# The stretch between the last logits and the expert products: written order, u and spp in halves, accumulators summed early

## The chip, the cores and the metric

The kernel runs on one core of a Trainium2 chip. The metric is the device time of one execution in microseconds. Three executions of the kernel before were timed and a further one was profiled; all times below that are points in the trace count from the profiled execution's first instruction. PE is TensorE's matmul, PEld its weight load, DVE VectorE, ACT ScalarE, POOL GpSimd, SP the engine whose queue issues every DMA here.

## The reference

Three layers follow each other in float32.

```python
# 1. attention, 4 x 8 heads x 576 x 64, local mask for heads 0-3, strided for 4-7 -> x (2304, 512)
# 2. h = x @ w_in;  g = h * sigmoid(1.702 h);  y = g @ w_out          (2304, 2048) and back
# 3. soft mixture of 8 experts with 4 slots each, on y:
logits = y @ phi                                  # (2304, 32)
d = softmax(logits, axis=0)                       # over tokens
slot_input = (d.T @ y).reshape(8, 4, 512)
slot_out[e] = maximum(slot_input[e] @ w1[e], 0) @ w2[e]        # 512 -> 1024 -> 512
c = softmax(logits, axis=1)                       # over slots
return c @ slot_out                               # (2304, 512)
```

The maximum over all tokens and the sum of the exponentials over all tokens are known only when the last token's logits are.

## The kernel before

The tokens are worked on in five chunks, four of 512 and a last one of 256. `moe_step` runs over 80 steps (c, f): chunk c, column block f of 128 of the 2048 hidden columns. A step makes `h` (12 matmuls in `gemm1`, L321), turns it into `g` with ACT and DVE (L324, L325) and transposes `g` in blocks of 32 with DVE (`g_transpose`, L348). The product with `w_out` is never made: `wp` is `w_out @ phi`, so the logits come from `g` directly (`logits`, L340, four f at a time, in four column tiles of 32), and `slot_input` is made as (d.T @ g) @ w_out.

`post(c)` keeps a running softmax over tokens. It copies the logits to `l4` (L388), sums and repeats them over the four column tiles with the matrix `rep` (`lr`, L391), takes the maximum (`nmx`, L393, L396), the exponentials (L402) and their block transposes `dT` (L404), the factor `al` by which earlier sums shrink (L408), and the running sum `z`. Then `u` = d.T @ g is made in four PSUM banks, one for each row group of 32 of PE, with 32x32 tiles (L435), and added into the accumulators `acc` with the factor `al` (L453). In the last chunk the four parts are not added into `acc`; they are copied out (L445), and `ut` sums old accumulators and new parts in PE with two weights, `selz[:, 1]` (selector times 1/z times `al`, L442) and `selz[:, 0]` (selector times 1/z, L446).

Behind that, at the end of the program: `ut` is transposed to `uts` (L590), `spp` is its product with `w_out`, which lies as 16 row blocks in `ex[0]` to `ex[3]` (L594), `acc_s` its copy in two halves (L596, L597), `sip` the sum over the four column tiles, transposed (L600), and `si` the slot inputs (L602). `expand1(G, n)` makes hidden columns of expert group G, 512 at a time, in four steps kt with the tiles `ex[4 + 8G + 4n + kt]` (L641), `hidden_t` transposes them (L652) and DVE spreads them into `hz` (L657). `expand2(half, n)` multiplies by the second expert weights `ex[20]` to `ex[35]` (L671) for three column ranges of 256, 128 and 128, `slot_out` splits the result, and `combine` multiplies it by the token weights (L688), copies the result out of PSUM (L691, L693) and issues the output DMA (L694).

The token weights are made by `combine_weights(c)` (L463 to L471: six DVE operations with one ACT exponential after the second), split by `combine_split` (L620, L621) and transposed by `combine_t` (`ctp`, L627, one transpose for each of 18 token blocks).

`load_ex` issues the 36 loads of 1 MB (L489) in a fixed order; each waits in SP's queue until the place it goes to is free. Before, nine of them go out at step (3, 2), two at (4, 1), two into places of `gT` at (4, 4), eight into places of `w_in` as its tiles are used up in chunk 4, one after the last step, and the rest from the u of the last chunk on, behind `spp` and the expert products that free their places.

Within these rules the order on each engine is found by a scheduler: among the instructions whose inputs are ready in its own simulation of the program it takes the one that was written first. `keep_busy(n)` issues n matmuls whose result nobody reads (L78).

## Time and profile before

| | |
|---|---|
| time, three executions | 438.43 us median (436.42 to 438.57) |
| time of the profiled execution | 439.01 us |
| span of the profiled execution | 437.1 us |
| mean granted TensorE clock | 0.985 |
| PE busy | 411.6 us (94%) |
| DVE, ACT, POOL busy | 263.6, 194.1, 77.5 us |
| HBM read, written | 71.34, 8.91 MB |

The span reaches from the first to the last instruction; 1.9 us of the profiled execution's time lie outside it. A granted clock of 1.00 is 2.4 GHz, 0.50 is 1.2 GHz. Busy time of PE is that of pipelined matmuls with modelled ends, so a busy PE is not a PE at its peak.

### The profile page before, as it was taken

To read this page: it belongs to the slowest core of one execution; us is meant where nothing else is said; L and a number is where in the kernel's file an instruction comes from. 1 tells how busy PE (TensorE), PEld (TensorE's weight loads), DVE (VectorE), ACT (ScalarE), POOL (GpSimd) and SP (SyncE) were. 2 spreads that over 40 slices of the span, in tenths; PEclk is the share of its full clock that TensorE was granted. 3 is DMA by queue.
4 is the path that set the end of the run, shared out by engine and by line. 5 is a ranking of instruction groups with operands and counts; after the bars stand their busy time and mean duration, and the time that the engine had idled before them with its cause. 6 is when DMAs were issued, how large, how long until landed. Compare 5 with 4: busy or idle time off the path is not lost.

```text
span 437.1 us, 10068 instructions
## 1 busy us (share of the span) xinstructions
PE 411.6 (94%) x4085; PEld 280.5 (64%) x4085; DVE 263.6 (60%) x564; ACT 194.1 (44%) x640; POOL 77.5 (18%) x96
## 2 busy tenths in 40 slices
PE   8978998998899999999999999999999999799992
PEld 4646575655467767777676776775777797243681
DVE  2789989998996555555557456546545465422141
ACT  3874867766664653555553436331221222220131
POOL 0454545454531110100110001000000000010000
PEclk9999999999989999999999999999999999899997
DMA  8957677676752130213411101693001899859998
GB/s 253 357 170 243 223 208 251 228 242 218 233 183 76 47 101 1 92 37 97 154 40 60 38 1 37 214 410 147 1 0 39 343 349 329 307 212 427 421 358 255
DMA packets 25614, 80.90 MB, mean 185 GB/s; under 512 B 2144, under 2 KB 9440, under 8 KB 21472
## 3 DMA queue, kind: packets, MB, share of 16 engines
q1 hardware_dynamic: 25568, 80.26, 52.5%
q8 instruction: 32, 0.52, 0.5%
q14 instruction: 14, 0.11, 0.1%
HBM read 71.34 MB, written 8.91 MB: 184 GB/s over the span
## 4 chain that ended last, share of the span: by engine, by line
PE 73%; DVE 8%; ACT 7%; POOL 4%; issue 3%; DMA 2%; SPq 0%; ACTq 0%; POOLq 0%; DVEq 0%
PE h L321 39%; PE u L435 5%; PE s L163 4%; PE lg L340 4%; PE op L671 4%; ACT ts L181 3%; PE hp L641 3%; PE ptp L199 3%; PE av L218 3%; DVE wc L264 2%; POOL ts L184 2%; PE fp L688 2%; POOL wc L262 2%; DVE wc L265 1%; DMA raw<-wraw 1%
## 5 line engine op out<-in xcount | busy, mean ns | idle before, releaser
L321 PE MATMUL h<-x,wi 128*128 128x512 f32 (+1 forms) x960 | 225.2, 381 | 4.3 <-POOL wi L273 1.7
L321 PEld LDWEIGHTS h<-x,wi 128*128 128x128 f32 x960 | 162.2, 189 | 53.8 <-issue 13.8
L325 DVE SCALAR_TENSOR_TENSOR gT<-gT,h 128x512 f32<-128x512 f32 (+1 forms) x64 | 40.6, 634 | 62.1 <-ACT gT L324 61.5
L324 ACT ACTIVATE gT<-h 128x512 f32<-128x512 f32 (+1 forms) x64 | 35.5, 555 | 68.2 <-PE h L321 66.6
L181 ACT ACTIVATE ts<-ts,nmx 128x64 f32<-128x64 f32 (+1 forms) x120 | 41.6, 349 | 28.6 <-DVE nmx L176 28.2
L184 POOL TENSOR_TENSOR ts<-ts,sm 128x384 f32<-128x384 f32 (+2 forms) x32 | 27.9, 872 | 139.2 <-DVE sm L183 65.5
L348 DVE STREAM_TRANSPOSE gT<-gT 128x512 f32<-128x512 f32 (+1 forms) x64 | 41.0, 649 | 0.9
L262 POOL TENSOR_SCALAR wc<-wc 128x512 f32<-128x512 f32 x32 | 25.0, 781 | 29.7 <-ACT wc L261 27.2
L340 PE MATMUL lg<-gT,wp 128*32 128x512 f32 (+1 forms) x128 | 27.2, 564 | 0.3 <-ACT wp L297 0.3
L264 DVE SCALAR_TENSOR_TENSOR wc<-raw,wc 128x512 uint32<-128x512 uint32 x32 | 26.0, 816 | 0.4
L263 DVE TENSOR_SCALAR wc<-wc 128x512 uint32<-128x512 uint32 x32 | 20.3, 635 | 7.9 <-POOL wc L262 7.9
L163 PE MATMUL s<-qk 64*64 64x96 f32 (+1 forms) x552 | 25.0, 235 | 0.0
L163 PEld LDWEIGHTS s<-qk 64*64 64x64 f32 x552 | 20.9, 133 | 6.3 <-issue 5.3
L243 ACT CAST x<-av 128x320 fp32r<-128x320 f32 (+20 forms) x54 | 19.1, 394 | 12.7 <-DVE x L244 9.1
L273 POOL TENSOR_TENSOR wi<-wc,wi 128x512 fp32r<-128x512 f32 x16 | 22.0, 1376 | 14.9 <-ACT wi L272 14.7
L265 DVE SCALAR_TENSOR_TENSOR wc<-raw,wc 128x512 uint32<-128x512 uint32 x32 | 24.4, 763 | 0.3
L261 ACT ACTIVATE wc<-raw 128x512 f32<-128x512 f32 x32 | 21.7, 678 | 4.3 <-DMA raw<-wraw 3.8
L182 DVE TENSOR_SCALAR sm<-sm 128x5 f32<-128x5 f32 (+2 forms) x32 | 6.8, 213 | 27.5 <-ACT ts L181 27.5
L435 PE MATMUL u<-gT,dT 32*32 32x512 f32 x576 | 21.0, 618 | 2.1 <-DVE z L410 2.1
L199 PE MATMUL ptp<-cs,ts 128*96 128x128 f32 (+1 forms) x120 | 18.2, 286 | 4.9 <-POOL ts L184 4.5
L181 ACT ACTIVATION_READ_ACCUMULATOR ts<-ts,nmx 128x1 f32 x120 | 22.6, 188 | 0.0
L699 POOL MEMSET hz<- 128x512 f32 x4 | 2.1, 560 | 112.1 <-PE spp L594 112.1
(124 smaller groups left out, 467.7 us busy)
## 6 DMA issues: line engine op xcount, KB each, us to landing
ex<-wexp SPq DMA_DIRECT2D x28, 1024.0 KB, 8.4
raw<-wraw SPq DMA_DIRECT2D x32, 512.0 KB, 4.2
qk<-lqk SPq DMA_DIRECT2D x8, 592.0 KB, 5.1
wo_scr<-wc SPq DMA_DIRECT2D x16, 256.0 KB, 2.8
ex<-wo_scr SPq DMA_DIRECT2D x4, 1024.0 KB, 9.2
gT<-wexp SPq DMA_DIRECT2D x4, 1024.0 KB, 7.0
qk<-sqk SPq DMA_DIRECT2D x6, 604.0 KB, 4.2
v<-lv SPq DMA_DIRECT2D x8, 432.0 KB, 4.8
```

The source lines that it names most:

```text
L163: nc.tensor.matmul(sp[hs, u], t[hs, qo:qo + 64], t[hs, ko + qo:ko + qo + nk], start=not early, stop=not early or u == nt - 1)
L181: nc.scalar.activation(ts[:, u], src[:, u], AF.Exp, scale=sc, bias=nmx[:, u:u + 1], accum_out=sm[:, u:u + 1])
L184: nc.gpsimd.tensor_tensor(ts, ts, sm[:, :nt].unsqueeze(2).to_broadcast([P, nt, nk]), op=ALU.mult)
L199: nc.tensor.transpose(ptp[:nk, u - a], src, ident)
L262: nc.gpsimd.tensor_scalar(t, t, F64_LARGE, F64_SMALL, op0=ALU.min, op1=ALU.max)
L264: nc.vector.scalar_tensor_tensor(u, raw[:, :, 1], 0xC0000000, u, op0=ALU.bitwise_and, op1=ALU.bitwise_or)
L321: nc.tensor.matmul(h[:, :N], w[:, we, 128 * kt:128 * kt + 128], x[xe][:, kt, :N], start=n == 0, stop=n == 11)
L324: nc.scalar.activation(g[:, :N], h[:, :N], AF.Tanh, scale=0.851)
L325: nc.vector.scalar_tensor_tensor(g[:, :N], g[:, :N], 1.0, h[:, :N], op0=ALU.add, op1=ALU.mult)
L340: nc.tensor.matmul(lgs[c][32 * j:32 * j + 32, :N], wp[:, f0 + j, :], gs[c, f0 + j][:, :N], start=f0 == 0, stop=f0 == NF - 4)
L348: nc.vector.transpose(t_slots(c)[:, f, :N], gs[c, f][:, :N])
L435: nc.tensor.matmul(us[a][32 * j:32 * j + 32, :].rearrange("p (t f) -> p t f", f=32), dT[q, 32 * b:32 * b + 32], gT[q, :, 32 * b:32 * b + 3 ...
```

## The change

The last chunk gets a function of its own, `post_last`, and `post` keeps the other four.

- At step (4, 6) `fold_acc` sums the four accumulators with `sel` into one bank `ua` and copies it to the place of `l4` and `dT`. The place of `acc` then takes a load (`load_ex(None, acc)`), so this load stands earlier in SP's queue and the last call that used to load the 36th tile loads nothing.
- From the last logits to `hidden_t(1, 0)` PE, DVE and ACT issue the instructions emitted in this region in the order in which they are written. Where instructions emitted outside of the region fall among them is left to the scheduler.
- `keep_busy(6)` behind the logits becomes 2 ahead of them, 1 ahead of `lr` and 4 ahead of `u`.
- `u` is made in two halves of 256 columns in eight banks. Each half is copied out, summed by `sel` into `ut_0` and `ut_1`, added to `ua` times `al` and transposed by DVE on its own.
- `spp` is made in two column halves, in the order given by `rows`. The factor 1/z moves from `selz` to the copies of `spp` (`scaled`). `sip` and `si` come in two halves; the second (`slot_in(1)`) is issued inside `expand1(0, 0)` behind kt = 0.
- `combine_weights(4)` and the split and transposes of chunks 0 and 1 stand in the region at the place where they are written, behind `hidden_t(0, 0)` and ahead of `expand1(1, 0)`; those of chunks 2 to 4 are written among `expand2(0, 5)` to `(0, 7)` as before.
- `uts`, `acc_s`, `c4t` and `cT0` have no tiles of their own any more; they lie in freed places.

```diff
-        if last:
-            zi = keep.tile([P, 1], F32, name="zi")
-            nc.vector.tensor_scalar(zi, st["z"], 1e-9, 2.0, op0=ALU.add, op1=ALU.mult)
-            nc.vector.reciprocal(zi, zi)
-            selz = keep.tile([P, 2, NS], F32, name="selz")
-            nc.vector.tensor_scalar_mul(selz[:, 0], sel, zi)
-            nc.vector.tensor_scalar_mul(selz[:, 1], selz[:, 0], al)
...
-            ut = mtile("ut")
-            for a in range(4):
-                nc.tensor.matmul(ut[32 * a:32 * a + 32, :], selz[:, 1], acc[:, a], start=True, stop=False)
-            for a in range(4):
-                u = slots[NF + a]
-                (nc.scalar.copy if a % 2 else nc.vector.tensor_copy)(u, us[a])
-                nc.tensor.matmul(ut[32 * a:32 * a + 32, :], selz[:, 0], u, start=False, stop=True)
-            st["ut"] = ut
-            return
...
+    def fold_acc():
+        st["l4"] = sp_["p"].tile([P, 512], F32, tag="l4", name="l4_last")
+        st["dT"] = sp_["p"].tile([P, 512], F32, tag="dT", name="dT_last")
+        ua = mtile("ua")
+        for a in range(4):
+            nc.tensor.matmul(ua[32 * a:32 * a + 32, :], sel, acc[:, a], start=True, stop=True)
+        st["ua"] = [st["l4"][:, 256:], st["dT"][:, 256:]]
+        for h in range(2):
+            nc.scalar.copy(st["ua"][h], ua[:, 256 * h:256 * h + 256])
+    def post_last():
+        c = len(CHUNKS) - 1
+        N = 256
+        ntt = 2
+        l4, dT = st["l4"][:, :N], st["dT"][:, :N]
+        nc.scalar.copy(l4, lgs[c][:, :N])
+        lr = mtile(f"lr_{c}")
+        keep_busy(1)
+        nc.tensor.matmul(lr[:, :N], rep, l4, start=True, stop=True)
+        nmx = keep.tile([P, 1], F32, tag="nmx", name=f"nmx_{c}", bufs=2)
+        nc.vector.tensor_reduce(nmx, lr[:, :N], axis=AX.X, op=ALU.max, negate=True)
+        nc.vector.tensor_tensor(nmx, nmx, st["nm"], op=ALU.min)
+        lp = mtile(f"lp_{c}")
...
+        keep_busy(4)
+        zp = keep.tile([P, 1], F32, tag="zp", name=f"zp_{c}", bufs=2)
+        nc.scalar.activation(l4, lr[:, :N], AF.Exp, bias=nmx, accum_out=zp)
+        nc.vector.transpose(dT, l4)
...
+        us = [mtile(f"u_{c}_{k}") for k in range(5)]
+        us += [ps_h.tile([P, 512], F32, tag="h", name=f"u_{c}_{k}") for k in (5, 6)]
+        us.append(ps_lg.tile([P, 512], F32, tag="lg", name=f"u_{c}_7"))
+        for h in range(2):
+            for i in range(2):
+                for a in range(4):
+                    for j in range(4):
+                        b = 4 * i + j
+                        q = slice(32 * a, 32 * a + 32)
+                        o = us[4 * h + a][32 * j:32 * j + 32, :256]
+                        nc.tensor.matmul(o.rearrange("p (t f) -> p t f", f=32), dT[q, 32 * b:32 * b + 32],
+                                         gT[q, 8 * h:8 * h + 8, 32 * b:32 * b + 32], start=i == 0, stop=i == 1)
+        uts = gt[0][:, NF].rearrange("p (t s) -> p t s", s=NS)
+        half = gt[0][:, NF + 1]
+        ut = []
+        for h in range(2):
+            for a in range(4):
+                (nc.scalar.copy if a % 2 else nc.vector.tensor_copy)(slots[NF + 2 + 2 * h + a // 2][:, 256 * (a % 2):256 * (a % 2) + 256], us[4 * h + a][:, :256])
+        for h in range(2):
+            ut.append(mtile(f"ut_{h}"))
+            for a in range(4):
+                nc.tensor.matmul(ut[h][32 * a:32 * a + 32, :256], sel, slots[NF + 2 + 2 * h + a // 2][:, 256 * (a % 2):256 * (a % 2) + 256], start=True, stop=True)
+            t = half[:, 256 * h:256 * h + 256]
+            nc.vector.scalar_tensor_tensor(t, st["ua"][h], al, ut[h][:, :256], op0=ALU.mult, op1=ALU.add)
+            nc.vector.transpose(uts[:, 8 * h:8 * h + 8].rearrange("p t s -> p (t s)"), t)
+        spp = [mtile(f"spp_{p}") for p in range(2)]
...
+        def rows(p, f0, f1):
+            for f in range(f0, f1):
+                j = f % 4
+                nc.tensor.matmul(spp[p][32 * j:32 * j + 32, :256], uts[:, f, :], ex[f // 4][:, f % 4, 256 * p:256 * p + 256], start=f < 4, stop=f >= NF - 4)
...
+        def scaled(p):
+            o = acc_s[:, 256 * p:256 * p + 256]
+            nc.vector.tensor_scalar_mul(o[:, :128], spp[p][:, :128], zi)
+            nc.scalar.mul(o[:, 128:], spp[p][:, 128:256], zi)
+        def slot_in(p):
+            sip = mtile(f"sip_{p}")
+            for k in range(2):
+                nc.tensor.matmul(sip[:, 32 * k:32 * k + 32], acc_s[:, 256 * p + 128 * k:256 * p + 128 * k + 128], sel, start=True, stop=True)
+            nc.vector.tensor_copy(si[:, 2 * p:2 * p + 2], sip[:, :64].rearrange("p (k s) -> p k s", s=NS))
+        rows(0, 0, 8)
+        rows(1, 0, 8)
+        rows(0, 8, 16)
+        scaled(0)
+        rows(1, 8, 12)
+        slot_in(0)
+        rows(1, 12, 16)
+        scaled(1)
+        return si, slot_in
...
         moe_step(i)
+        if (c, f) == (4, 6):
+            fold_acc()
+            load_ex(None, acc)
...
+    man = ctx.enter_context(ExitStack())
+    man.enter_context(tc.manual_schedule(engines={mybir.EngineType.PE, mybir.EngineType.DVE, mybir.EngineType.Activation}))
+    keep_busy(2)
     logits(c, NF - 4)
-    keep_busy(6)
-    for _ in post(c):
-        pass
-    ut = st["ut"]
-    acc_es.close()
+    si, slot_in = post_last()
...
-    spp = mtile("spp")
-    for f in range(NF):
-        j = f % 4
-        nc.tensor.matmul(spp[32 * j:32 * j + 32, :], uts[:, f, :], ex[f // 4][:, f % 4, :], start=f < 4, stop=f >= NF - 4)
-    acc_s = tl.tile([P, DM], F32, name="acc_s")
-    nc.vector.tensor_copy(acc_s[:, :256], spp[:, :256])
-    nc.scalar.copy(acc_s[:, 256:], spp[:, 256:])
-    sip = mtile("sip")
-    for kt in range(4):
-        nc.tensor.matmul(sip[:, 32 * kt:32 * kt + 32], acc_s[:, 128 * kt:128 * kt + 128], sel, start=True, stop=True)
-    si = tl.tile([P, 4, NS], F32, name="si")
-    nc.vector.tensor_copy(si, sip[:, :128].rearrange("p (k s) -> p k s", s=NS))
...
             w = ex[4 + 8 * G + 4 * n + kt]
+            if G + n == 0 and kt == 1:
+                slot_in(1)
...
     hidden_t(1, 0)
+    man.close()
     for n in range(8):
         expand2(0, n)
```

## Rows read from the trace of the kernel before

**Rows 1.** Stretches: us, PE busy (instructions), granted clock, DMA share, GB/s.
```profile
350.00:369.20 19.20, 19.20 (x166) 1.00 0.94 346
372.75:374.80 2.05, 0.00 (x0) 1.00 1.01 404
...
376.40:379.50 3.10, 3.10 (x39) 0.50 0.47 106
...
387.80:391.80 4.00, 4.00 (x39) 1.00 0.01 4
392.00:418.00 26.00, 26.00 (x362) 1.00 1.00 414
418.00:434.00 16.00, 10.65 (x192) 0.90 1.07 338
```

**Rows 2.** The chain that ended last, in order of time: start, us, what.
```profile
374.85 3.18 PE u L435 x62
...
381.61 3.64 PE spp L594 x32
...
388.25 7.00 PE hp L641 x64
395.25 0.58 PE hT L652 x4
...
404.16 2.73 PE op L671 x48
```

**Rows 3.** Timeline from the last activation tile to u: start, us, instruction [idle before].
```profile
369.73 0.42 DVE L325 SCALAR_TENSOR_TENSOR gT<-gT,h 128x256 f32<-128x256 f32 x1 [0.54 <-ACT gT L324]
369.77 0.82 PE L78 MATMUL busy<-cs 128*128 128x512 bf16 x3
...
370.52 0.62 PE L340 MATMUL lg<-gT,wp 128*32 128x256 f32 x2
...
372.40 0.42 DVE L393 TENSOR_REDUCE nmx<-lr 128x1 f32<-128x256 f32 x1 [1.76 <-PE lr L391]
...
373.66 0.47 ACT L402 ACTIVATE l<-lr,nmx 128x256 f32<-128x256 f32 x1 [0.69 <-DVE ca L465]
...
374.26 0.45 DVE L404 STREAM_TRANSPOSE dT<-l 128x256 f32<-128x256 f32 x1 [0.77 <-ACT l L402]
```

**Rows 4.** Timeline of PE, the first chunk's u.
```profile
158.86 4.46 PE L435 MATMUL u<-gT,dT 32*32 32x512 f32 x128
```

**Rows 5.** A stretch of 0.2 us as the last u begins, columns as in rows 1.
```profile
374.80:375.00 0.20, 0.15 (x16) 1.00 1.16 492
```

**Rows 6.** Timeline after u: durations of the kinds of instruction that the tail issues.
```profile
381.48 0.45 DVE L620 CAST c4t<-ca 128x256 fp32r<-128x256 f32 x2
...
381.85 0.76 DVE L621 TENSOR_TENSOR c4t<-ca,c4t 128x256 fp32r<-128x256 f32 x2
...
385.18 0.53 PEld L627 LDWEIGHTS ctp<-cs,c4t 128*128 128x128 f32 x5 [0.84 <-issue]
...
385.32 0.42 DVE L596 COPY acc_s<-spp 128x256 f32<-128x256 f32 x1 [2.72 <-PE spp L594]
...
395.99 0.61 DVE L657 COPY hz<-hT 128x64 f32<-128x64 f32 x4
```

**Rows 7.** Timeline, token weights of the last chunk.
```profile
374.31 0.24 ACT L466 ACTIVATE ca<-ca 128x64 f32<-128x64 f32 x1
...
375.39 0.22 DVE L471 TENSOR_TENSOR ca<-ca,cz 128x64 f32<-128x64 f32 x1
```

**Rows 8.** Timeline, SP's queue and the last evacuation.
```profile
428.77 4.01 SPq L694 DMA_DIRECT2D out<-gT  x5
...
429.57 0.37 ACT L691 COPY gT<-fp 128x256 f32<-128x256 f32 x1 [0.19 <-PE fp L688]
```

**Rows 9.** DMA issues on the page: KB each, median us from issue to landing.
```profile
wo_scr<-wc SPq DMA_DIRECT2D x16, 256.0 KB, 2.8
...
out<-gT SPq DMA_DIRECT2D x9, 256.0 KB, 5.1
```

More of the change, by code (lines that the diff above doesn't have):

```diff
@@ L385, in post @@
         ntt = N // 128
-        first, last = c == 0, c == len(CHUNKS) - 1
+        first = c == 0
         l4 = sp_["p"].tile([P, 512], F32, tag="l4", name=f"l4_{c}")
@@ L424, in post @@
         yield
-        if not last:
-            yield
+        yield
         us = [mtile(f"u_{c}_{a}") for a in range(4)]
@@ L436, in post @@
                                      gT[q, :, 32 * b:32 * b + 32], start=i == 0, stop=i == nb // 4 - 1)
-        if c < 4:
-            taken.difference_update(range(NF))
-        if last:
-            ut = mtile("ut")
-            for a in range(4):
-                nc.tensor.matmul(ut[32 * a:32 * a + 32, :], selz[:, 1], acc[:, a], start=True, stop=False)
-            for a in range(4):
-                u = slots[NF + a]
-                (nc.scalar.copy if a % 2 else nc.vector.tensor_copy)(u, us[a])
-                nc.tensor.matmul(ut[32 * a:32 * a + 32, :], selz[:, 0], u, start=False, stop=True)
-            st["ut"] = ut
-            return
+        taken.difference_update(range(NF))
         for a in range(4):
@@ L454, in post @@
         yield
-        if not last:
-            combine_weights(c)
+        combine_weights(c)
+    def fold_acc():
[7 more added lines that the diff above has]
+            nc.scalar.copy(st["ua"][h], ua[:, 256 * h:256 * h + 256])
@@ new lines, in post_last @@
+    def post_last():
[11 more added lines that the diff above has]
+        lp = mtile(f"lp_{c}")
+        for tt in range(ntt):
+            nc.tensor.matmul(lp[:, 32 * tt:32 * tt + 32], l4[:, 128 * tt:128 * tt + 128], sel, start=True, stop=True)
+        keep_busy(4)
+        zp = keep.tile([P, 1], F32, tag="zp", name=f"zp_{c}", bufs=2)
+        nc.scalar.activation(l4, lr[:, :N], AF.Exp, bias=nmx, accum_out=zp)
+        nc.vector.transpose(dT, l4)
+        al = keep.tile([P, 1], F32, tag="al", name=f"al_{c}", bufs=2)
+        nc.scalar.activation(al, st["nm"], AF.Exp, scale=-1.0, bias=nmx)
+        z = keep.tile([P, 1], F32, tag="z", name=f"z_{c}", bufs=2)
+        nc.vector.scalar_tensor_tensor(z, st["z"], al, zp, op0=ALU.mult, op1=ALU.add)
+        zi = keep.tile([P, 1], F32, name="zi")
+        nc.vector.tensor_scalar(zi, z, 1e-9, 2.0, op0=ALU.add, op1=ALU.mult)
+        nc.vector.reciprocal(zi, zi)
+        L = keep.tile([P, 4, NS], F32, tag="L", name=f"L_{c}")
+        nc.scalar.copy(L[:, :ntt], lp[:, :N // 4].rearrange("p (t s) -> p t s", s=NS))
+        st["L"] = L
+        gT = t_slots(c)
+        us = [mtile(f"u_{c}_{k}") for k in range(5)]
[28 more added lines that the diff above has]
+                nc.tensor.matmul(spp[p][32 * j:32 * j + 32, :256], uts[:, f, :], ex[f // 4][:, f % 4, 256 * p:256 * p + 256], start=f < 4, stop=f >= NF - 4)
+        acc_s = half
+        si = keep.tile([P, 4, NS], F32, name="si")
+        def scaled(p):
[16 more added lines that the diff above has]
+        return si, slot_in
@@ L554, in tile_kernel @@
             acc = accp.tile([P, 4, 512], F32, name="acc")
-            more = accp.tile([P, 3, 512], F32, name="more")
+            more = accp.tile([P, 3, 512], F32, tag="more", name="more")
             slots.update({NF + 3 + k: more[:, k] for k in range(3)})
@@ L611, in tile_kernel @@
     c4s = {}
+    cT = sp_["p"].tile([P, 3, 512], F32R, tag="more", name="cT")
+    cTs = [cT[:, k] for k in range(3)] + [sp_["p"].tile([P, 512], F32R, tag="l4", name="cT3")]
     def combine_split(c):
@@ L615, in combine_split @@
         ntt = N // 128
-        t = c4t[:, c % 2]
+        t = gt[0][:, NF if c % 2 else NF + 2]
         c4s[c] = t
@@ L627, in combine_t @@
             nc.tensor.transpose(ctp[:, 128 * tt:128 * tt + 128], c4s[c][:, 128 * tt:128 * tt + 128], ident)
-        nc.scalar.copy(cT0[:, c0:c0 + N] if c < 4 else cT1, ctp[:, :N])
+        nc.scalar.copy(cTs[c] if c < 4 else cT1, ctp[:, :N])
     hzt = e1p.tile([P, 2, 8, P], F32, tag="e", name="hz")
@@ L687, in combine @@
                 tok = P * (k + t)
-                nc.tensor.matmul(fp[:, t - a], cT0[:, tok:tok + P] if k + t < 16 else cT1[:, tok - 2048:tok - 2048 + P], so[:, 1, c0:c0 + w], start=True, stop=True)
+                nc.tensor.matmul(fp[:, t - a], cTs[(k + t) // 4][:, P * ((k + t) % 4):P * ((k + t) % 4) + P] if k + t < 16 else cT1[:, tok - 2048:tok - 2048 + P], so[:, 1, c0:c0 + w], start=True, stop=True)
             obs[0] = not obs.get(0)
```

6 lines of the change are left out of this document (removed).

## The prediction

> **What bounds the kernel now.** First the stretches of time, to see which engine is full where. In chunk 4, from 350 to 369.2 us, PE is busy 19.20 of 19.20 us [rows 1]: whatever is added to PE there is paid in full. Then the chain of waits, in order of time. From the last activation tile to the first expert product it hops from engine to engine: u begins at 374.85, spp at 381.61, the first expert product at 388.25, and from there on PE is again the chain almost alone [rows 2]. The change is made in these hops, so each must be priced on its own.
>
> The third view is the granted clock. In 372.75 to 374.80 PE does nothing at all; afterwards, from 376.4 to 379.5, the clock stands at 0.50, which is 1.2 GHz, in the middle of u and ut, while the stretches before it read 1.00 [rows 1]. So part of the hop from u to spp is paid at half speed. The three times lie 2.15 us apart (436.42 to 438.57); a fall that some executions have and some don't would be of that size, but the times alone don't show it.
>
> The last view is DMA. It is nearly idle from 387.8 to 391.8 (share 0.01) because the loads wait for the expert products to free their places; from 392 to 434 it is full (1.00, then 1.07), while PE's last work is over by 430 [rows 1]. The last copy out of PSUM ends at 429.57 + 0.37 = 429.94, but SP is still issuing the five last output DMAs until 428.77 + 4.01 = 432.78 [rows 8]. A 256 KB output takes 5.1 us to land, a 256 KB write earlier in the program 2.8 [rows 9]. So the end itself hangs on a DMA backlog behind PE, and the reader should carry two questions: what PE gains, and what the backlog gives back.
>
> **The change, part by part** (gain negative, against the profiled execution's 439.01).
>
> (1) `fold_acc`. Four matmuls of 512 columns, two passes each, in four column tiles: the same kind as 8 of spp's 32, which take 3.64 [rows 2], so 0.91. PE has no gap there [rows 1], so **+0.9** (0.8 to 1.0). The two ACT copies lie beside PE work.
>
> (2) Last logits to u. The last activation tile is ready at 369.73 + 0.42 = 370.15, but its logits start at 370.52, behind three busy matmuls of 0.82 in all [rows 3]. With two of them, and ahead of all four logits, PE is free at 370.15; some 0.1 for the hand-off, and 0.28 is gained. Next, the maximum's reduction ends at 372.82 and the exponential starts at 373.66, 0.84 later, with the token-weight operations of DVE between (its releaser is named as `ca` L465) [rows 3]. In written order only the minimum stands there: about 0.3, a gain of 0.54. Exponential and transpose (0.47, 0.45) stay. Together **-0.8**; -0.4 if the exponential's late start is ACT's own.
>
> (3) u to spp. Before 381.61 - 374.85 = 6.76 [rows 2]. After: u has 128 matmuls of half the columns in place of 64. In the first chunk 128 of full width took 4.46 [rows 4]; if columns set the pace, 128 half-wide ones take 2.23, the first half being ready at about 1.2. Each engine copies two tiles per half, 0.42 each [rows 6], overlapped: the second half's are done at about 3.0, and DVE is then free for the first half's sum (0.42, as the row of L325) and transpose (0.45) [rows 3]. With two hand-offs spp starts at 3.97, so **-2.8**. The second half's sum and transpose (0.9 more) hide behind the first 16 of `rows`, which is 1.8 of spp's 3.64. The four busy matmuls fill 1.0 of PE's pause ahead of u and cut it from 2.05 to about 0.5, so I take u at full clock. If the clock falls as before, half of about 3.1 us comes back: +1.5.
>
> Is it columns that set the pace? In the 0.2 us stretch where the last u begins, 16 matmuls are under way within 0.15 us, so one every 10 ns or faster [rows 5]; I take columns. The Trainium skill (the page "TensorE: Matmul & The Clock Gate", section "Wait — 56ns, not 53.3ns?") says that start to start of matmuls never drops below about 25 ns however few their columns; by it the 128 would take 3.2 us and the sum be 1.0 worse. The trace does not agree for these packed 32x32 tiles.
>
> (4) spp to the first expert product. Before 388.25 - 381.61 = 6.64 [rows 2], with 15 of the 18 `ctp` transposes in it (0.53 for five, so 0.106 each, 1.6 in all) [rows 6]. After: spp's columns are the same, 3.4 until PE is free; then one half of sip (4 weight loads, 0.44) lies ahead of the product, and scaling, half of sip and si for the first half hide behind `rows(1, 8, 12)` and `(1, 12, 16)` but for some 0.4. 4.25, so **-2.4** (-2.0 to -2.6). The other half of sip is inside the product: **+0.4**.
>
> (5) The written order behind `hidden_t(0, 0)`. What waits here is PE itself. `combine_weights(4)` now stands on DVE behind the copies to `hz`, which ended 396.60 - 395.25 = 1.35 after the hT transposes began [rows 2, 6]. Then six small DVE operations of about 0.22, one ACT exponential of 0.24 and two hand-offs of 0.1, 1.75 [rows 7]; a split is half of 0.45 + 0.76, 0.6 [rows 6]. So the first of the four `ctp` can start 3.8 after hT began, where PE was done with hT at 0.58. Four transposes, the second split's remainder, four more: `expand1(1, 0)` starts at about 5.0 in place of 0.58: **+4.4**. The token weights cost PE nothing before, since they were spread over DVE's idle time from 373 on. This wait takes back most of what (2) to (4) give.
>
> The stall has a possible filling. `expand2(0, 0)` and `(0, 1)` need only what `hidden_t(0, 0)` made; they are written outside of the region, so the scheduler may put them into PE's gap, and in the program before it did the like with the `ctp` between spp and sip. Two such groups are 32 of the 48 matmuls in 2.73, 1.8 us [rows 2], ready at 1.45 and over by 3.3. I take them as filled, **-1.8** (bound: 0).
>
> (6) Ten transposes of chunks 2 to 4 come among `expand2(0, n)` where three did: 7 x 0.106 = **+0.7**.
>
> (7) The load in the place of `acc`. One load of 1.05 MB fewer in the late run of DMA, at 414 GB/s [rows 1] 2.5; and that run starts about 4.7 earlier, because the first expert products free its places (5.1 by (1) to (4), less the half of sip inside). The loads end near 411 in place of 418, and the first outputs, which PE sets, come behind them. Earlier DMA runs at 0.94 up to 369 [rows 1], and the added load lands later in it, in the pause behind 376.4 (share 0.47); nothing waits for it. Then the last output DMA is issued as its copy ends, some 0.6 after 429.94 and not 2.84, and lands faster: **-2.1** (0 to -2.6).
>
> Sum: 0.9 - 0.8 - 2.8 - 2.4 + 0.4 + 4.4 - 1.8 + 0.7 - 2.1 = **-3.5**. PE itself gains only 1.4 of it; the rest is backlog. On the profiled execution 435.5; that one lies 0.58 above the median of the three, so the forecast for the median is **435.0** (434.9 rounded up).
>
> **The rivals.** A change of less than 0.5% (2.2 us, so 436.2 to 440.6) is about what a measurement of this kernel can't tell from none.
>
> - A, as above, 435.0: chance 0.56. For it: the sum; its own spread is 433.0 to 436.5.
> - B, nothing fills the stall of (5): -3.5 + 1.8, 436.7. For it: `expand2` stood behind all of `hidden_t` before; against it: there was no gap on PE then. 0.12.
> - C, the backlog gives nothing back, because the outputs alone fill DMA to the end (1.07 in 418 to 434 [rows 1]): only PE's 1.4, 437.0. Then giving the place of `acc` to a load buys nothing. Against it: DMA would have no loads left by then, and the copies that free the last outputs are spread over PE's last products. 0.10.
> - D, slower: the unfilled stall, 3.2 us, is longer than the pause of 2.05 behind which the clock fell [rows 1]. If it falls here, expert products run at 1.2 GHz, and each stretch like the one of 3.1 us costs 1.55. The first brings B's time to 438.3, no change; the second decides, 439.8 and slower than before; the third, 441.4, is past the bound. For it: the one fall that the trace shows; against it: the filling cuts the stall into pauses of 0.9 and 0.5, and PE came back to 1.00 behind that one stretch. 0.11, of which 0.05 past the bound.
> - E, the number of matmuls and not their columns sets u's pace: then 128 take 4.46 at half the columns too [rows 4], and spp starts 2.2 later: 437.1. Rows 5 speak against it [rows 5]; the rule of the skill above is a milder form of it. 0.05.
> - F, the hops are shorter than I took them, above all (5), because token weights and splits overlap more: 432.8. 0.06.
>
> Faster by over 0.5%: 0.49 of A and all of F, 0.55. Slower by over 0.5%: 0.05 of D and 0.03 for a place in the written order where PE waits and that I have not seen, 0.08. The rest, 0.37, is no change. The range reaches from the good end of A, which is F's, to D's first stretch and a little beyond: 432.8 to 438.8.
>
> **What would show it.** (1) PE still full to the last logits, these some 0.9 later. (2) u about 0.8 sooner behind the last L325. (3) Granted clock 1.00 through u; spp about 4.0 behind u's start. (4) The first expert product 4.2 behind spp. (5) On PE between the first hT and the second group's products a gap ended by DVE's split, with or without `op` in it, and the clock behind it. (7) DMA idle ahead of the first output; the last output issued within 1 us of the last copy. The forecast is wrong if the gap in (5) is much longer than 3.2 us or drags the clock down, or if the last output stays late although the loads end early.

## The result, and the profile after

| | before | after | forecast |
|---|---|---|---|
| time, median (19 executions each, side by side) | 438.26 us (436.42 to 439.86) | 441.53 us (439.45 to 443.97) | 435.0 (432.8 to 438.8) |
| ratio to before, 95% interval | | 1.0071 [1.0055, 1.0088] | |
| time of the profiled execution | 439.01 us | 439.71 us | 435.5 |
| its span | 437.1 us | 437.9 us | |
| its mean granted clock | 0.985 | 0.995 | |

The change makes the kernel 0.7% slower; 435.0 was forecast. Two different misses add up to that. The profiled execution after is 0.70 us longer than the one before where -3.5 was forecast, and it lies 1.82 us below the median of its kernel, while the profiled execution before lay 0.75 above. 0.70 + 1.82 + 0.75 = 3.27, the difference of the medians.

First the profiled execution. The chain of waits of the changed kernel, in order of time (start, length, what; the line numbers are those of the changed kernel):

```profile
354.81 0.99 PE ua L442 x8
...
375.04 2.83 PE u L487 x115
377.87 0.56 PE ut L498 x7
378.43 1.85 issue
380.28 0.82 PE ut L498 x9
381.11 0.65 issue
381.76 3.23 PE spp L507 x56
...
385.02 0.81 PE sip L520 x4
385.83 0.57 PE spp L507 x8
386.40 0.86 PE hp L705 x8
...
397.13 0.43 DVE gT L683
397.57 0.04 issue
397.62 0.66 PE ctp L689 x4
...
398.94 3.57 PE hp L705 x32
```

Two rows stand out. In the middle of `ut`, behind its seventh matmul, PE stands still for 1.85 us, and "issue" says that nothing the profile knows of held it. (The 0.65 ahead of `spp` is no such riddle: from 380.70 to 381.66 DVE adds and transposes the first half.) Later `ctp` starts at 397.62, and it is DVE, with the split of the token weights (L683), that the chain follows there. The timeline of the same stretch shows all that DVE does between, with the idle time ahead of each group and what ended it in brackets:

```profile
393.89 0.66 PE L716 MATMUL hT<-cs,hc 128*128 128x128 f32 x4
394.09 0.69 DVE L708 TENSOR_SCALAR hc<-hp 128x512 f32<-128x512 f32 x1 [6.01 <-PE hp L705]
394.70 0.61 DVE L721 COPY hz<-hT 128x64 f32<-128x64 f32 x4
395.22 0.21 DVE L538 TENSOR_REDUCE cm<-L 128x2 f32<-128x64 f32 x1
...
396.67 0.23 DVE L546 TENSOR_TENSOR ca<-ca,cz 128x64 f32<-128x64 f32 x1
...
397.62 1.32 PE L689 MATMUL ctp<-cs,gT 128*128 128x128 f32 x8 [3.06 <-DVE gT L683]
```

Before the token weights, DVE had stood idle for 6.01 us, waiting for an expert product; the weights need only the logits. They are made where they are written, and PE waits 3.06 us for them. No `op` stands in that gap.

By stages, each the difference of two starts in the chain of before [rows 2, 3, 8] or of after, and the last one from the last copy's end (429.94, and 433.03 + 0.37 = 433.40) to the end of the span:

| stage | before | after | change | forecast |
|---|---|---|---|---|
| last g ready at | 370.15 | 371.33 | +1.18 | +0.9, (1) |
| last g to u | 4.70 | 3.71 | -0.99 | -0.8, (2) |
| u to spp | 6.76 | 6.72 | **-0.04** | -2.8, (3) |
| spp to the first expert product | 6.64 | 4.64 | -2.00 | -2.4, (4) |
| expert product (0, 0) to (1, 0) | 7.59 | 12.54 | **+4.95** | +3.0, (4), (5) |
| (1, 0) to the last copy's end | 34.10 | 34.46 | +0.36 | +0.7, (6) |
| last copy's end to the end of the span | 7.16 | 4.50 | -2.66 | -2.1, (7) |
| sum | | | +0.80 | -3.5 |

The two stages in bold miss their forecast by 2.76 and 1.95; the others together come out 0.4 better than theirs.

### The profile page after: what moved, and what is told of

The parts are those of the page before. It is cut to its first block, busy times and chain, and to the rows that moved or that the text cites. A ratio compares the mean times of both kernels' runs of the same rounds, so it can differ in the third digit from the quotient of the medians.

```text
span 437.9 us, 10285 instructions
## 1 busy us (share of the span) xinstructions
PE 411.8 (94%) x4185; PEld 282.0 (64%) x4190; DVE 265.9 (61%) x569; ACT 195.7 (45%) x645; POOL 78.2 (18%) x96
## 4 chain that ended last, share of the span: by engine, by line
PE 69%; DVE 9%; ACT 7%; issue 5%; POOL 5%; DMA 4%; SPq 0%; ACTq 0%; POOLq 0%; DVEq 0%
PE h L321 37%; PE u L426 4%; PE s L163 4%; PE lg L340 4%; ACT ts L181 4%; PE op L735 4%; PE hp L705 3%; DVE wc L264 3%; PE ptp L199 3%; PE av L218 2%; DMA raw<-wraw 2%; DMA qk<-lqk 2%; POOL wc L262 2%; POOL ts L184 2%; DVE wc L265 2%
## 5 line engine op out<-in xcount | busy, mean ns | idle before, releaser
L262 POOL TENSOR_SCALAR wc<-wc 128x512 f32<-128x512 f32 x32 | 26.0, 812 | 28.9 <-ACT wc L261 26.4
L264 DVE SCALAR_TENSOR_TENSOR wc<-raw,wc 128x512 uint32<-128x512 uint32 x32 | 26.7, 836 | 0.4
L265 DVE SCALAR_TENSOR_TENSOR wc<-raw,wc 128x512 uint32<-128x512 uint32 x32 | 24.7, 771 | 0.3
L263 DVE TENSOR_SCALAR wc<-wc 128x512 uint32<-128x512 uint32 x32 | 20.3, 635 | 7.4 <-POOL wc L262 7.3
L203 ACT COPY pt<-ptp 96x384 f32<-96x384 f32 (+1 forms) x34 | 15.0, 483 | 14.7 <-PE ptp L199 14.6
```

The lines of the kernel that those rows point to most:

```text
L262: nc.gpsimd.tensor_scalar(t, t, F64_LARGE, F64_SMALL, op0=ALU.min, op1=ALU.max)
L264: nc.vector.scalar_tensor_tensor(u, raw[:, :, 1], 0xC0000000, u, op0=ALU.bitwise_and, op1=ALU.bitwise_or)
L265: nc.vector.scalar_tensor_tensor(u, raw[:, :, 0], 29, u, op0=ALU.logical_shift_right, op1=ALU.bitwise_or)
```

## The experiments

**The stall ahead of ctp.** `weights_early` moves the token weights and the first two splits ahead of `expand1(0, 1)`, where DVE is idle; the transposes stay.

```diff
+    combine_weights(4)
+    for c in range(2):
+        combine_split(c)
     expand1(0, 1)
...
     hidden_t(0, 0)
-    combine_weights(4)
     for c in range(2):
-        combine_split(c)
         combine_t(c)
```

> combine_weights(4) and the splits of chunks 0 and 1 are written behind expand1(0, 0) and not behind hidden_t(0, 0); the transposes stay. Theory (the pause of 3.06 us between hT and ctp is only DVE's order): it vanishes, expand1(1, 0) starts about 3.1 us earlier against the first product, and the end comes 2.5 to 3.1 us earlier, 438.4 to 439; more, up to 4.5, if the clock often falls behind that pause in the changed kernel. Rival (the end is set by DMA, whose loads and outputs would then meet again): less than 1.5 us.

Measured: 436.35 us median, ratio to before 0.9961 [0.9933, 0.9989], so 1.1% (4.8 us) below the changed kernel's 1.0071, a little more than the 4.5 that the theory allowed. The chain:

```profile
377.74 1.70 issue
...
385.55 0.86 PE hp L705 x8
...
393.12 0.59 PE hT L716 x4
393.70 0.87 PE ctp L689 x8
394.58 3.57 PE hp L705 x32
```

The stall is gone, and expert product (0, 0) to (1, 0) is 9.03 in place of 12.54: between these two profiles the stall cost 3.51. The median fell by more; falls of the clock that come with the stall in a part of the executions (below) would make up the rest, which is inferred. The pause in `ut` is still there, 1.70. `order_ends_early` leaves every line where it is and closes the region of written order ahead of `hidden_t(0, 0)`.

```diff
+    man.close()
     hidden_t(0, 0)
...
     hidden_t(1, 0)
-    man.close()
```

> The changed kernel with the region of written order closed ahead of hidden_t(0, 0) in place of behind hidden_t(1, 0); nothing else. Theory: the stall of 3.06 us ahead of ctp is made by the written order alone, since the six token-weight operations and the splits need nothing later than the logits; the scheduler may then put them into DVE's idle time from 373 on, expert product (1, 0) starts 20.3 us behind dT and not 23.9, and the time falls by 3 to 3.7 us against the changed kernel, to a ratio of 0.998 to 1.000, unless the operations come ahead of the copies of u or the spp scaling and delay those: each 0.2 us of DVE on the path then costs as much, up to 1.2 us in all. Rival, the prediction's step (5): the scheduler fills the stall with expand2(0, 0) and (0, 1) instead and leaves the weights where they are; then op stands between hT and ctp, and 1.8 us are gained, ratio 1.003.

Measured: 437.02 us, 0.9976 [0.9953, 1.0]. Freed of the order, the scheduler puts the six operations among those for `z` and `zi` on DVE, ahead of the copies of `u`, and `hT` and expert product (1, 0) follow each other 1.02 apart (397.43 and 398.45). `op` isn't moved: its first matmuls stand behind the `hT` of (1, 0) here too. In its profiled execution the 20.3 us is not seen (23.73): the pause in `ut` is 2.54 there and spp takes 4.97 at a fallen clock, while the splits stand between spp and the first expert product. That the order alone made the stall held, and the filling that step (5) counted on did not come here either. `no_order` removes the region altogether.

```diff
-    man.enter_context(tc.manual_schedule(engines={mybir.EngineType.PE, mybir.EngineType.DVE, mybir.EngineType.Activation}))
```

> The changed kernel without the region of written order: the scheduler places PE's, DVE's and ACT's instructions in the tail. It puts the token weights among the operations of the last logits and the busy matmuls ahead of lr. If the region's order is worth what step (2) and the spp part of steps (3) and (4) say, the hop from the last g to u is 0.5 to 0.9 us longer than in the changed kernel and spp to hp some 0.3 to 0.6, while the stall of 3.06 us is gone: in sum 1.5 to 2.5 us faster than the changed kernel, ratio 1.001 to 1.004. Rival: the written order buys nothing but the stall, and the time is that of the region that ends early, ratio 0.996 to 0.999.

Measured: 437.21 us, 0.998 [0.9953, 1.0008], the time of the rival. From u to expert product (1, 0) it takes 20.27 us in its profile, `weights_early` 20.23. What the order gains between spp and hp (4.64 against 5.21 here) the scheduler gains elsewhere. From the last g to u it takes 4.32 here and 3.71 in the changed kernel, so the 0.6 that the order gains there is real, as the theory had it; in the median, 437.21 against the 436.35 of `weights_early`, the two intervals overlap.

**The pause in ut.** `shift128` replaces four of the seven busy matmuls at the start of the program, 370 us ahead of the tail, by 68 tiny ones, which makes PE's stream 128 instructions longer. The tail is the same.

```diff
-    keep_busy(7)
+    keep_busy(3)
+    pad = ps_h.tile([P, 512], F32, tag="h", name="pad")
+    for _ in range(68):
+        nc.tensor.matmul(pad[:32, :16], busy[:, :32], busy[:, :16], start=True, stop=True)
```

> The tail is the changed kernel's, word for word; only at the program's start 4 of the 7 idle busy matmuls are replaced by 68 of 16 columns, so PE's instruction stream is 128 instructions longer ahead of everything else. Theory 1 (the pause of 1.85 us inside ut, 378.43 to 380.28, which no wait explains, is PE waiting for its own next instructions, and it comes at that place because u's 256 instructions pass in 2.4 us): the pause moves or vanishes, spp starts some 4.9 us behind u's start in place of 6.72, the expert products and the end come about 1.8 us earlier, 439.7. Rival (the pause is a wait for the copies of u or for a place in PSUM that the trace does not name): the same pause at the same matmul, 441.5.

Measured: 439.3 us, 1.0021 [1.0001, 1.004], 0.5% below the changed kernel. The chain has no pause, and spp starts 4.61 us behind u in place of 6.72, so the pause cost 2.11:

```profile
376.80 2.83 PE u L490 x114
379.63 1.25 PE ut L501 x16
380.88 0.53 issue
381.41 3.23 PE spp L510 x56
```

The same pad in the kernel before is the control.

> The kernel before, with four of the start's busy matmuls replaced by 68 tiny ones of 16 columns, as in the run with the shifted instruction stream; nothing else. If the shift helped the changed kernel only because it moves a place where PE waits for its own instructions out of u and ut, there is nothing to move here: the ratio to the kernel before is 0.997 to 1.003, some 438.3 us. Rival: the tiny matmuls are worth something anywhere, at the start or for the clock, whatever kernel they stand in: then the 2.2 us that they took off the changed kernel come off here too, 436.1 us, ratio 0.995.

Measured: 438.48 us, 1.0003 [0.998, 1.0026]: the pad does nothing by itself. A longer pad, `pause_moved`, should have put the pause into `spp`.

```diff
-    for _ in range(68):
+    for _ in range(100):
```

> The changed kernel with 100 tiny matmuls in the place of four busy ones at the start, so that PE's stream is 192 instructions longer ahead of the tail (the earlier run had 128). Theory, PE waits for its own instructions, which come in blocks of about 256: the place where a block ends is now 64 instructions behind the one in the changed kernel, so ut runs without a pause and a pause of 0.3 to 1.9 us, with no releaser that the profile knows, stands in spp, near its 23rd matmul; time between the other shift's ratio and the changed kernel's, 1.002 to 1.007. Rival 1, ut waits for something of its own (a copy, a tile): the pause of 1.85 us stays behind ut's seventh matmul, ratio 1.007. Rival 2, any tiny matmuls at the start remove the pause: none in u, ut and spp, ratio 1.002.

Measured: 445.0 us, 1.0137 [1.0091, 1.0183]. This expectation failed. There is no pause in u, ut or spp (u to spp is 4.61 again), so the place of a pause can't be had by counting blocks; and the time is far above all three forecasts. A part of that the chain shows further on:

```profile
399.38 1.97 PE ctp L692 x8
401.35 5.56 PE hp L708 x32
```

The same 8 transposes took 1.32 and the same 32 matmuls 3.57 in the changed kernel's profile: here the clock fell (its granted clock is 0.87 over 400 to 420), which is 2.64 us. More on that below. Another part lies ahead of the tail: u begins at 378.92, and at 375.04 in the changed kernel's profile. Why is open. The next two runs change the number of instructions itself. `u_whole` makes u as the kernel before does, in 64 matmuls of 512 columns:

```diff
-    for h in range(2):
-        for i in range(2):
-            for a in range(4):
-                for j in range(4):
+    for i in range(2):
+        for a in range(4):
+            for j in range(4):
...
-                        o = us[4 * h + a][32 * j:32 * j + 32, :256]
+                    nc.tensor.matmul(us[a][32 * j:32 * j + 32, :].rearrange("p (t f) -> p t f", f=32), dT[q, 32 * b:32 * b + 32],
+                                     gT[q, :, 32 * b:32 * b + 32], start=i == 0, stop=i == 1)
```

> The changed kernel with u written as the kernel before has it, in 64 matmuls of 512 columns and four tiles, each half copied from its half of the tile; the rest is the changed kernel's. Theory: the pause of 1.85 us in ut comes from the 256 instructions of u passing in 2.4 us, faster than PE's instructions are loaded; with half as many it is gone, u takes 2.2 to 2.4 us, the first half's copies wait for all of it, and spp starts 4.2 to 4.6 us behind u's start in place of 6.72: ratio to the kernel before 1.000 to 1.004. Rival 1, the pause has another cause and stays: 6.1 to 6.7 us, ratio 1.007. Rival 2, the halves are worth what the prediction's step (3) gave them, since copies then start 1 us later: no pause, but 5.0 us or more, ratio 1.003 to 1.005.

Measured: 438.94 us, 1.0026 [1.0001, 1.0051]. No pause; the timeline of PE:

```profile
376.58 2.35 PE L483 MATMUL u<-gT,dT_last 32*32 32x512 f32 x64 [0.64 <-DVE dT_last L465]
379.33 0.59 PE L494 MATMUL ut<-gT,cs 128*32 128x256 f32 x3 [0.41 <-ACT gT L490]
...
381.34 1.02 PE L503 MATMUL spp<-ex,gT 128*32 128x256 f32 x13 [0.48 <-PE ut L494]
```

u to spp takes 4.76, a little over the 4.2 to 4.6 of the theory, and only 0.15 more than the two halves without their pause. `u_quarters` goes the other way, to four quarters of 64 matmuls of 128 columns.

```diff
-        for h in range(2):
+        for h in range(4):
...
-                        o = us[4 * h + a][32 * j:32 * j + 32, :256]
+                        o = us[4 * (h // 2) + a][32 * j:32 * j + 32, 128 * (h % 2):128 * (h % 2) + 128]
...
-                                         gT[q, 8 * h:8 * h + 8, 32 * b:32 * b + 32], start=i == 0, stop=i == 1)
+                                         gT[q, 4 * h:4 * h + 4, 32 * b:32 * b + 32], start=i == 0, stop=i == 1)
```

> The changed kernel with u in four quarters of 64 matmuls of 128 columns in place of two halves of 64 matmuls of 256; copies and the rest are the changed kernel's. Theory: PE waits for its own instructions when many short ones stand together; 512 instructions in place of 256 give more of it: pauses with no releaser of 2 us and more in sum within u and ut, and u takes 256 x 22 ns = 5.6 us without them (128 matmuls took 2.83), since below some 256 columns it is the number of matmuls that sets the pace. Rival: columns set the pace and the pause has nothing to do with the number of instructions: u 2.3 to 2.9 us and one pause of 1.9 us or none.

Measured: 444.02 us in one execution, a span of 442.2, and on PE's timeline:

```profile
373.49 2.01 PE L487 MATMUL u<-gT,dT_last 32*32 32x128 f32 x135 [0.64 <-DVE dT_last L465]
377.79 2.76 PE L487 MATMUL u<-gT,dT_last 32*32 32x128 f32 x121 [2.28 <-issue]
```

The pause stands behind the 135th matmul of u. In the changed kernel it stands behind 128 of u and 7 of ut: again 135. It comes at the same instruction, whatever that instruction computes and whatever tile it reads. A cause in the data is out. The forecast of 5.6 us for u was wrong: 135 matmuls passed in 2.01, 14.9 ns each.

**The clock.** `busy_in_stall` fills the stall with 12 busy matmuls behind `hidden_t(0, 0)`.

```diff
     hidden_t(0, 0)
+    keep_busy(12, mtile("hold"))
     combine_weights(4)
```

> 12 busy matmuls of 512 columns (2.6 us) fill the pause between hT and ctp and delay nothing. Theory (in a part of its executions the clock falls behind that pause, which spreads the times from 439.5 to 444): median falls to 439.7 to 440.3, spread under 2 us, clock 1.00 to the last products. Rival (the spread has another cause): 441.5 with the same spread.

Measured: 440.9 us, 1.0057 [1.0036, 1.0078]; five executions within 439.8 to 441.8, none near the 442 to 444 that the changed kernel also has. The stall as such stays (12.54 between the expert products) and the clock stays at 1.00 behind it. This settles little: the median is above the 439.7 to 440.3 of the theory, the interval overlaps the changed kernel's, 11 of whose 19 executions lie below 441.8 too, and its first profile has no fall either. Two further executions of the changed kernel as it is show what its first profile doesn't.

> The changed kernel once more, with a profile. Seven of its 19 executions lie within 439.45 to 440.13 us, the profiled one among them, the other twelve at 441.03 to 443.97. Theory: in those the clock falls behind the stall of 3.06 us ahead of ctp, as two other kernels with that stall show (the 32 matmuls of expert product (1, 0) take 5.27 and 5.56 us in place of 3.57): if this execution is above 441 us, its expert product (1, 0) takes 5 us or more and the granted clock between 390 and 400 is below 1.00. Rival: the difference lies ahead of the tail (the clock at 30 to 40 and 100 to 150 us, which the kernel before shows too): the last g is 1.3 us or more later than 371.33 and the tail behind it runs as in the first profile.

> As the look before it: above 441 us either the expert product (1, 0) behind the stall takes 5 us or more, or the last g is 1.3 us or more later than 371.33; below 440.2 us neither.

Measured: 442.9 and 442.59 us, spans of 441.1 and 440.8. The chain of the first of them:

```profile
377.40 2.56 issue
379.96 1.28 PE ut L498 x9
381.23 0.23 issue
381.47 4.25 PE spp L507 x56
...
398.34 1.97 PE ctp L689 x8
400.31 5.44 PE hp L705 x32
```

and its stretches of time (PE busy and matmuls, PEld, DVE, ACT, POOL, then granted clock, DMA share, GB/s):

```profile
379.00:380.00 1.00, 0.04 (x4) 0.04 (x6) 0.00 (x0) 0.00 (x0) 0.00 (x0) 1.00 0.85 336
...
382.00:383.00 1.00, 1.00 (x16) 0.54 (x12) 0.22 (x1) 0.00 (x0) 0.00 (x0) 0.50 0.56 229
...
396.00:398.30 2.30, 0.00 (x0) 0.00 (x0) 1.81 (x10) 0.26 (x1) 0.00 (x0) 0.77 1.05 442
398.30:400.00 1.70, 1.66 (x8) 1.57 (x8) 1.08 (x4) 0.45 (x1) 0.00 (x0) 0.50 0.96 405
...
402.00:404.00 2.00, 2.00 (x16) 0.54 (x12) 0.00 (x0) 0.00 (x0) 0.00 (x0) 0.50 0.97 410
```

The clock falls to 0.50, which is 1.2 GHz, twice: at the end of the pause, which is 2.56 here and not 1.85, and in the last part of the stall, so that the work behind both runs at half speed. Against the first profile that is 0.71 for the longer pause, 1.02 in spp, 0.65 in ctp and 1.87 in expert product (1, 0), 4.25 in all; the last logits came 1.03 earlier (the chain has their copy at 371.01, in the first profile at 372.04), and the span is 3.2 longer. The second shows the same two falls (spp 4.47, ctp 1.97, product 5.56). So rival D's mechanism is at work in these executions. That the other executions above 441 us have the same is inferred; they have no profile.

**The load in the place of acc.** One line is left out, so that each later load takes the next place:

```diff
         if (c, f) == (4, 6):
             fold_acc()
-            load_ex(None, acc)
```

> The changed kernel without the expert load in the place of the accumulators; every later load takes the next place. In the changed kernel DMA moves nothing between 418 and 420 us, ahead of the outputs, and the span ends 4.50 us behind the last copy out of PSUM, where the kernel before has 7.16. If the prediction's step (7) holds for it, the load of 2.5 us more comes out of that end: 6.0 us or more. Rival, as the faster version showed: the load fits into the idle time ahead of the outputs and the end stays at 4.4 to 5.0 us; then the place of the accumulators bought nothing, and the backlog went because PE sets the outputs later.

Measured: 439.94 us in one execution, a span of 438.2, the last copy over at 433.44 + 0.37 = 433.81, so 4.39 from there to the end; the changed kernel has 4.50. The stretches show where the extra load went, first those of the changed kernel,

```profile
416.00:417.00 1.00, 1.00 (x22) 0.44 (x14) 0.00 (x0) 0.56 (x3) 0.00 (x0) 1.00 0.21 66
...
419.00:420.00 1.00, 1.00 (x22) 0.86 (x24) 0.58 (x1) 0.81 (x2) 0.00 (x0) 1.00 0.00 0
```

then those without the load:

```profile
417.00:418.00 1.00, 1.00 (x34) 0.83 (x36) 0.49 (x1) 0.67 (x2) 0.00 (x0) 1.00 0.70 287
...
419.00:420.00 1.00, 1.00 (x17) 0.81 (x13) 0.17 (x1) 0.41 (x1) 0.00 (x0) 1.00 0.00 0
```

DMA's loads end some 1.5 us later and it is idle at 419 all the same. The time is that of the rival; its reason, PE's later outputs, is taken up below. In the faster version (below) the same line was taken out as well.

> The version with the token weights written early and the shifted stream, without the expert load in the place of the accumulators; every later load then takes the next place, as in the kernel before. The prediction's step (7): one load of 1.05 MB more in the late run, 2.5 us of DMA, stands ahead of the outputs, and the end comes up to 2.1 us later: 436.5 us, the span's end 6.4 us behind the last copy out of PSUM in place of 4.3. Rival: what ended the backlog was the earlier start of the late loads, and the outputs have room enough to catch up (DMA moves 205 to 233 GB/s between 422 and 428 there); then the load's place is worth under 0.5 us: 434.5 to 435.0 us, the end 4.3 to 4.8 us behind the last copy.

Measured: 434.77 us, 0.9921 [0.9891, 0.9952]; with the load it is 434.45. The end is 4.8 behind the last copy, with the load 4.3. The rival, both times: in the time of the kernel the load's place gives nothing that can be measured.

**Both losses removed.** `weights_early_shift` is `weights_early` and `shift128` together.

> Both edits. If the two pauses add: 4.3 to 5 us under the changed kernel, 436.5 to 437.2, and faster than the kernel before. If one hides behind the other or DMA takes over the end: no better than the better of the two alone by 0.7 us.

Measured: 434.45 us, 0.992 [0.9896, 0.9943]. The two losses add, 1.5% below the changed kernel where the single edits gave 1.1% and 0.5%; the time is lower than the 436.5 to 437.2 expected. The same without the pad, but with u in one go, which doesn't hang on where an instruction happens to lie:

> u in one go and the token weights and first two splits ahead of expert product (0, 1), no shift of the stream. If the two losses are separate (the pause in ut, 2.1 to 2.5 us, and the stall ahead of ctp, 3.7 us), both go: 433.8 to 435.2 us, ratio 0.990 to 0.993, as with the shifted stream. Rival: without the shift the pause stays or comes back elsewhere: 436 us and over, ratio 0.995 or more.

Measured: 434.36 us, 0.9912 [0.9878, 0.9946], the best of all here: 0.9% below the kernel before and 1.6% below the changed one. u to expert product (1, 0) takes 18.43 us in its profile, 20.99 before and 23.90 after. One small piece of it, the scaling of spp on DVE alone:

```diff
-            nc.vector.tensor_scalar_mul(o[:, :128], spp[p][:, :128], zi)
-            nc.scalar.mul(o[:, 128:], spp[p][:, 128:256], zi)
+            nc.vector.tensor_scalar_mul(o, spp[p][:, :256], zi)
```

> The same, with each half of spp scaled by DVE alone in one operation of 256 columns in place of one of 128 on DVE and one of 128 on ACT. In the changed kernel ACT's half starts only when DVE's is over, and spp to the first expert product takes 4.64 us where 4.25 were forecast. Theory: the wait is between the two halves of one tile, so one operation is shorter than the two in a row: 4.2 to 4.4 us from spp to hp, 0.2 to 0.4 us less in all, too little for the time to tell. Rival: the wait is for the tile of spp itself or for the hop to PE, and nothing moves or DVE's longer operation costs: 4.6 to 4.8 us.

Measured: 434.46 us, 0.9915 [0.9884, 0.9946]; spp to the first expert product 4.60 against 4.64. Nothing is gained, as its rival said.

## Why the prediction was wrong

**(1) and (2) were right**: +0.99 for `fold_acc` (354.81) against 0.9, and -0.99 against -0.8. The front is some 0.2 later besides, which is little against what it varies by from one execution to the next: u begins at 375.04, 374.00 and 373.39 in the three profiles of the changed kernel.

**(3) failed.** It forecast -2.8 and the profile has -0.04. Of the 2.76, 2.11 are the pause (6.72 against the 4.61 of `shift128`), which no step had. 0.6 are the term for u itself: the step took half-wide matmuls at half the time, 2.23, and they took 2.83. 64 of 512 columns take 2.35 (36.7 ns each), 128 of 256 take 2.83 (22.1 ns), 128 columns cost 14.9 ns: the time falls with the columns, but not in proportion. The 16 matmuls in 0.15 us of [rows 5], by which the step chose the columns, are a burst at the start that u doesn't keep up. So the premise of rival E, a fixed time for each matmul, is refuted, but a milder one, that half the columns cost more than half the time, is right for 0.6 us. The Trainium skill ("TensorE: Matmul & The Clock Gate", section "Wait — 56ns, not 53.3ns?") says that start to start never drops below about 25 ns; the trace shows 22.1 and 14.9 for these packed tiles. What the step promised for making u in two halves is nearly nothing: 4.61 without the pause against 4.76 in one go.

The pause is one of PE's own instruction stream: it stands at the same instruction in kernels with different work there, it is gone when the stream is shifted or u has half the matmuls, and the trace's DMA records have a 16 KB instruction load beginning at 378.03, 0.88 us long, just as PE stands still, the first of its size since 358.84. The records of the other runs fit. In all eight profiled executions in which PE stands still behind its 135th matmul, its next one starts 2.24 to 2.42 us after such a load begins, whether the pause is 1.04 long (`busy_in_stall`: load at 378.12, PE at 380.40) or 2.56 (`changed_look_1`: 377.66 and 379.96). And PE stops when 500 to 513 of its matmuls and weight loads are on record since the beginning of the load before; in the nine tails without the pause the next load begins after 439 at most. (`no_order` stops for 1.09 behind the 136th matmul, with the load 2.35 before it goes on; there the view names DVE.) That this late load is what PE waits for is still inferred; no view names a releaser. The Trainium skill ("Runtime: NRT & Kernel Launch", section "Instruction fetch mechanics") has instructions refilled in blocks of 16 KB, the crossing "mostly hidden". The block size agrees with the trace; if the inference holds, this crossing was not hidden, for 1.04 to 2.56 us. Why the load comes so late here stays open. In `pause_moved` the load before begins later, at 366.90, and the next one begins behind 439 instructions, in time by the same count.

**(4) was right within 0.4**: -2.00. By the chain, 3.23 + 0.03 + 0.81 + 0.57 = 4.64 lie between spp and the first expert product. `sip` and the wait for the scaling are the 0.84 that the step gave them; the two parts of spp take 3.80 where it took 3.4. ACT's half of the scaling starts after DVE's, but doing it on one engine gave nothing.

**(5) failed in its filling.** The stall itself was worked out to 0.05 us (`hT` at 393.89, expert product (1, 0) at 398.94: 5.05 for 5.0). The -1.8 for `expand2` moved into it by the scheduler did not come, and in none of the runs, with the region or without, did `op` stand ahead of the `hT` of (1, 0). Why the scheduler left the gap open no run shows. With 0 in its place the sum is -1.7, which was rival B. What spoke for B was misread, though: in the kernel before, `op` starts at 404.09 and the last `hT` at 406.82, so `expand2` did not stand behind all of `hidden_t`, only behind the first three.

**(6) was smaller**, +0.36 for 0.7.

**(7) had the size, but the load's place has next to no part in it.** The end gave back 2.66 for 2.1, and without the load in the place of `acc` it does so too. What goes with it, and is taken for the cause, is how long DMA has been done with the loads when the last copy out of PSUM ends. In the trace's DMA records a load's packets have 8 KB and an output's 1 KB or less. In the kernel before the last load packet ends at 422.87 (the step took 418), 7.07 us ahead of the last copy; in the changed kernel at 417.54 (the step took 411), 15.9 ahead, and without the load in the place of `acc` at 418.94, 14.9 ahead. The run of loads starts only 1.28 earlier (390.69 for 391.97) where the step took 4.7. PE is later as well: with the stall and the pause SP issues the first output at 419.80, and in the kernel before at 415.66. That lateness is not needed: in `weights_early_shift`, with neither, the first output is issued at 414.60, the loads end at 415.81, 12.4 ahead of the last copy, and the end is 4.34 behind it. Without the load in the place of `acc` it is 9.4 and 4.8 there, so the place has a small part where the distance is short.

```profile
419.80 14.98 SPq L758 DMA_DIRECT2D out<-gT  x15
```

**Rival D was undervalued**, at 0.11 and 0.05 past the bound. The sum was made on one execution, in which the clock held after as it did not before. In both further profiles it fell with the unfilled stall, in the first for 0.65 + 1.87 = 2.5 us, more than the 1.55 of a stretch that D counted with, and with the pause besides. Roughly, B's 436.7 with such a fall, the 2.1 of the pause and the 0.6 of u is 441.9, and the median is 441.53.

## What to carry to other kernels

A written order fixes not only the chain that it was written for, but also the side work that the scheduler had spread over idle time: work that needs only early results belongs where its engine is idle, not ahead of its consumer. Counting instructions belongs to the price of a split: halving matmuls saves less than half the time for each, and many short ones in a row can bring PE to a stop that no wait in the program explains, as `u_whole` shows by having none. A stall on PE is not priced by its length alone, since the clock may fall behind it, in some executions and not in others, so one profile without a fall is no proof.

## What the runs showed of the hardware

- PE can stand still for 1.04 to 2.56 us with no releaser, at the same place of its instruction stream, behind 135 matmuls with their weight loads that had passed in 2.0 to 3.4 us. It went on 2.24 to 2.42 us after the beginning of a 16 KB instruction load, in eight profiled executions.
- The stall of 3.06 us went with a fall of the clock, which began in it or up to 1.4 us behind it, in `changed_look_1`, `changed_look_2`, `u_whole`, `u_quarters`, `pause_moved` and `changed_noload`, and not in the first profile of the same kernel or in `shift128`. So its length alone doesn't decide. Of the pauses in u and ut, those of 2.28, 2.54 and 2.56 us went with a fall, those of 1.04, 1.17, 1.70 and 1.85 did not.
- A packed 32x32 matmul took 36.7, 22.1 and 14.9 ns on average at 512, 256 and 128 columns (`u_whole`, the changed kernel, `u_quarters`, at a granted clock of 1.00).
